# A product-key expert layer mixed with a 2-D Fourier filter: the index of a maximum for two slots at once, three more groups summed on TensorE, fewer loads, a planner with measured figures

## Chip, cores, metric

One core of one Trainium2 chip runs the whole kernel. The metric is device microseconds (us) of one execution. The kernel before takes 991.58 us, the median of 3 runs (990.01 to 991.66).

## The reference, cut to what matters

```python
def _A_ref(x, w_r, w_i):                      # x: 1 x 2048 x 576
    X = rfft2(x) * (w_r + 1j * w_i)
    return irfft2(X)

def _B_ref(x, w_q, k1, k2, u, v):             # 32 heads, 64 x 64 experts
    q = einsum("nd,dhc->nhc", x, w_q)
    s1 = einsum("nhd,ed->nhe", q[..., :128], k1)
    s2 = einsum("nhd,ed->nhe", q[..., 128:], k2)
    e = argmax(s1) * 64 + argmax(s2)          # one expert for each token and head
    act = gelu(einsum("nd,nhd->nh", x, u[e]))
    return einsum("nh,nhd->nd", act, v[e])    # softmax over one candidate is 1

g = sigmoid((x * gate_w).sum(-1))
return g * _A_ref(x, ...) + (1 - g) * _B_ref(x, ...)
```

Inputs and output are float32. Which of the 4096 rows of u and v a token needs is known only after its scores: 2048 tokens x 32 heads x 4608 bytes (a row of u beside a row of v) = 302 MB are gathered.

## The kernel before, in words

The tokens lie in 16 tiles of 128, the heads in 8 chunks of 4. Tiles 0 to 9 (`E_T`) are called early here, tiles 10 to 15 late.

**Scores, 64 slots.** A slot is one chunk and two tiles (`scores`, L402). TensorE (PE) multiplies the transposed x by a matrix that holds w_q times the keys (`build_m`, L381; both are split in a high and a low part, so 28 matmuls of 128 x 512 a slot). VectorE (DVE) takes the maximum of each 64 scores (L427). ScalarE (ACT) makes the sign of maximum minus score (L435), which is 0 at the maximum and 1 elsewhere, and adds 0, 1/4, 2/4 or 3/4 by quarter (L446). DVE then finds the place of the 0: minimum of the two halves (L448, 128 x 512 bf16), of the two quarters (L448, 128 x 256), plus a ramp (L449), minimum over the 16 places left (L451), and the two indices together (L454); ACT writes the row number into `ei` (L455). Each slot does these steps by itself.

**Groups.** A group is one tile and one chunk: 4 gathers (`group`, L480; L487, issued by GpSimd, POOL) fetch 128 rows of 4608 bytes each into a ring of `NG` = 12 buffers, and later also a ring of `NG2` = 1. DVE makes four dot products with x (L496), ACT the gelu (L500), DVE the weights a (L501). The sum over the v rows is done by DVE (L512, L514), or, where `is_d` says so, by PE: ACT writes a diagonal matrix for each weight (L524), PE multiplies it by the v rows (8 matmuls of 128 x 288 a group, two records each in the profile), and DVE or ACT takes the sum out of PSUM (L540, L538). On PE are tiles 1, 4, 8 for chunks 0 to 6, and tiles 10, 12, 14 for all chunks. The 80 early groups run beside the scores, the 48 late ones beside the Fourier part.

**Fourier part.** It starts when the memory of the scores is free (`switch`, L621): 16 folds (L645: symmetric and antisymmetric halves of each row on DVE, then PE), 9 units over frequencies (`unit`, L784: f2 and f4 on PE, the multiplication by w on DVE, L709 to L712, f6 on PE, back into the table `bt` on DVE, L775 to L782), then 16 inversions (`invert`, L808: 6 matmuls of width 289 with `fi`, a copy on ACT, 4 with `krb`), scaled by the gate on ACT (L830, L831) and mixed with the expert sum on DVE (L835).

**Who sets the order.** All instructions are jobs of a planner (`Plan`, L105). Each job has an engine, a guessed duration and a due time; the planner simulates the engines, takes the earliest due job that is ready and has its buffers, and the result is the fixed order of every engine's instructions. On the chip every engine runs its list strictly in order. The due times hang on `TPS` (us for a slot), `LE` (how many slots a group lies behind the scores), `TGS` (pace of late groups) and `FPACE` (pace of the Fourier part). A group may only be placed behind the slot that makes its indices (L601).

Of the kernel before, what the change touches and what calls it, by code (L numbers as in the profile page):

```python
# [32 lines left out]
def _tables():  # L33
# [19 lines left out]
    fwd = np.stack([  # L53
        rows(np.cos, np.arange(0, 128)), rows(np.cos, np.arange(128, 256)), ct,
        -rows(np.sin, np.arange(0, 128)), -rows(np.sin, np.arange(128, 256)), -st,
    ])
    ck = np.full(DF, 2.0)
    ck[0] = ck[-1] = 1.0
    ck /= S * D

    def irows(fn, ks):
        return fn(2 * np.pi * np.outer(ks, k) / D) * ck[ks][:, None]

    ct = z.copy()
    ct[:33] = irows(np.cos, np.arange(256, 289))
    st = z.copy()
    st[64:96] = irows(np.sin, np.arange(256, 288))
    inv = np.stack([
        irows(np.cos, np.arange(0, 128)), irows(np.cos, np.arange(128, 256)), ct,
        irows(np.sin, np.arange(0, 128)), irows(np.sin, np.arange(128, 256)), st,  # L70
# [173 lines left out]
def pe(n):  # L244
    return max(0.25, n * 0.0018)
# [7 lines left out]
def tile_kernel(ctx, tc, xn, xT, wqT, kT, wri, uv, gw, t_kr, t_fi, t_f4, t_f6, t_io, out):  # L253
# [30 lines left out]
    for tag, n in (("cand", 3), ("z", 8), ("b", 8), ("a", 8), ("im", 2), ("fe", 2), ("dg", 4)):  # L284
        ring(tag, "sm", n)
# [3 lines left out]
    for tag, n in (("mh", MB), ("ml", MB), ("mx", 2), ("sg", 2), ("kT", 1), ("ramp", 1)):  # L289
        ring(tag, "sp", n)  # L290
# [65 lines left out]
    def load_x(b, i, at, at2):  # L356
        st = buf("uv", ROW, view=lambda x: x[:, 0, :512])
        ld(load(P * 2048, 2048), at, lambda: nc.sync.dma_start(st.ap, xT[:, i, b * 512 : b * 512 + 512]), [st])
        hi = xts[i if i < 4 else 8][b]
        lo, r = (xts[4 + i][b], 0) if i < 4 else (hi, 64)  # L360
        ac(act(512), at2, lambda: actv(hi.ap, st.ap, AF.Copy), [hi], [st])
        dv(dve(512), at2, lambda: vt(lo.ap[r:], st.ap[r:], hi.ap[r:].bitcast(F32), ALU.subtract), [lo], [st, hi])
# [37 lines left out]
    score_jobs = {}  # L400

    def scores(c, tp, at):  # L402
# [44 lines left out]
        for wd in (E // 2, E // 4):  # L447
            dv(0.07 + wd * 16 / 1920, at, lambda wd=wd: vt(s2()[:, :, :wd], s2()[:, :, :wd], s2()[:, :, wd : 2 * wd], ALU.min), [sg], [])  # L448
        dv(0.2, at, lambda: vt(s2()[:, :, :Q], s2()[:, :, :Q], ramp.ap[:, :Q].unsqueeze(1).to_broadcast([P, 4 * HPC, Q]), ALU.add), [sg], [ramp])  # L449
        im = buf("im", [P, 2, HPC, 2])  # L450
        dv(0.34, at, lambda: nc.vector.tensor_reduce(  # L451
            im.ap.rearrange("p a h b -> p (a h b)"), s2()[:, :, : E // 4], AX.X, ALU.min), [im], [sg])
        fe = buf("fe", [P, 2, HPC])
        dv(0.08, at, lambda: stt(fe.ap, im.ap[:, :, :, 0], float(E), im.ap[:, :, :, 1], op0=ALU.mult, op1=ALU.add), [fe], [im])  # L454
        ac(0.18, at, lambda: actv(ei[tp][:, :, 4 * c : 4 * c + 4], fe.ap, AF.Copy, scale=float(E)), [("ei", tp, c)], [fe])  # L455
# [24 lines left out]
    def group(t, c, at, ahead, gate_by=()):  # L480
        rows = []
        for k in range(HPC):
            g = buf(("uv", "uv2"), ROW)
            h = c * HPC + k

            def go(g=g, h=h):
                on("POOL", nc.gpsimd.indirect_dma_start(  # L487
                    out=g.ap.rearrange("p a d -> p (a d)"), out_offset=None, in_=uv,
                    in_offset=bass.IndirectOffsetOnAxis(ap=ei[t // 2][:, t % 2, h : h + 1], axis=0)))
# [89 lines left out]
    for s in range(NCH * 8):  # L579
# [65 lines left out]
    def fold(t, at):  # L645
        x = xs[t]
        f = buf("f5", [P, ND * P])
        ac(0.17, at, lambda: actv(f.ap[:, 0:385:384], x.ap[:, 0:1].to_broadcast([P, 2]), AF.Copy), [(f, 0)], [x])  # L648
# [15 lines left out]
    def f2(q, at):  # L664
        p = psum()

        def go():
            for r in range(2):
                for n, i in enumerate(((0, 1, 2), (3, 4, 2))[r]):
                    mm(p.ap[:, r, :DF], BT.ap[:, i, :, q], fi[0].ap[:, 3 * r + n, :], start=n == 0, stop=n == 2)  # L670

        plan("PE", 6 * pe(DF), at, go, [p], [fi[0], (BT, "q", q)] + [(BT, "in", t, i) for t in range(NT) for i in range(2)])
# [4 lines left out]
    def turns(k, at):  # L677
        t4 = buf("t4", [P, 3, P])
        t6 = buf("t6", [P, 5, P])
        ld(load(P * 1024, 1024), at - 8, lambda: nc.sync.dma_start(t4.ap[:, 0:2, :], t_f4[k]), [(t4, 0)])  # L680
# [249 lines left out]
```

## Time and profile before

| | |
|---|---|
| median of 3 runs | 991.58 us |
| the profiled execution's own time | 1001.24 us |
| its span, first to last instruction | 999.5 us |
| busy: PE, DVE, ACT, POOL | 90%, 92%, 51%, 57% of the span |
| mean granted clock of PE | 0.965 |
| moved by DMA | 348.39 MB, of it 302.02 MB gathers |
| first gather issued, last gather issued | 36.67 us, 979.74 us |
| scores end on PE, first fold on PE | 601.8 us, 628.6 us |
| first inversion on PE | 862.7 us |

The profiled execution took 1.0% longer than the median. Where a row of the profile says "x16 | 13.5, 751 | 1.6", the group has 16 instructions, was busy for 13.5 us, one of them took 751 ns, and its engine was idle for 1.6 us just before them. In a timeline a row gives the start, the length, the engine, the line, and in brackets how long the engine had been idle and what ended that. DVE overlaps the end of one instruction with the start of the next, so what one costs in a full queue is read from start to start and not from its length.

### The profile page before, as it was taken

How to read it: one execution, taken by the hardware profiler on the slowest of the kernel's cores; microseconds unless marked ns; L12 is line 12 of the kernel's file. 1: busy time of each engine (PE TensorE's matmuls, PEld its weight loads, DVE VectorE, ACT ScalarE, POOL GpSimd, SP SyncE). 2: the span in 40 equal slices, each digit the busy share in tenths (PEclk: the TensorE clock that was granted, in tenths of full speed). 3: DMA queues.
4: the chain of work that ended last, by engine and by line, in shares of the span. 5: the costliest groups of instructions: out<-in, count | busy, mean ns of one | idle time of the engine just before them, and what ended most of it. 6: DMA issues, size and time to landing. Idle time of an engine off the chain costs nothing. (4 is left out here: it accounts for less than half of the span.)

```text
span 999.5 us, 14406 instructions
## 1 busy us (share of the span) xinstructions
PE 904.4 (90%) x4208; PEld 735.8 (74%) x4208; DVE 916.7 (92%) x2255; ACT 514.6 (51%) x1877; POOL 574.4 (57%) x516
## 2 busy tenths in 40 slices
PE   8997999999999999999998990777999998899993
PEld 7885888878877888887877880665777776677762
DVE  3996999999999999999999999999999999977776
ACT  3874676676666576676666664522212222233331
POOL 0354656565656565755657566476655565676662
PEclk9997999999999999999999996889999999899998
DMA  9987999998989999998999799889999999999994
GB/s 336 336 286 301 349 361 367 358 352 305 392 309 361 371 344 332 395 345 328 386 360 330 291 394 378 340 312 389 394 357 351 357 353 321 349 390 414 398 359 192
DMA packets 93246, 348.39 MB, mean 349 GB/s; under 512 B 10480, under 2 KB 13296, under 8 KB 93168
## 3 DMA queue, kind: packets, MB, share of 16 engines
q0 software_dynamic: 73728, 302.02, 80.9%
q1 hardware_dynamic: 19440, 45.45, 12.3%
q8 instruction: 34, 0.56, 0.2%
q14 instruction: 44, 0.36, 0.1%
HBM read 342.71 MB, written 4.72 MB: 348 GB/s over the span
## 5 line engine op out<-in xcount | busy, mean ns | idle before, releaser
L487 POOL DMA_INDIRECT uv<-uv,ei x512 | 574.2, 1121 | 406.2 <-PE p L313 133.3
L313 PE MATMUL p<-mh,xt 128*128 128x512 f32 x1152 | 383.3, 402 | 9.1 <-ACT sg L435 7.3
L435 ACT ACTIVATE sg<-p,mx 128x64 bf16<-128x64 f32 x1024 | 225.8, 352 | 78.1 <-DVE mx L427 55.7
L514 DVE SCALAR_TENSOR_TENSOR xn<-uv,a,xn 128x576 f32<-128x576 f32 x322 | 262.0, 814 | 1.5
L313 PEld LDWEIGHTS p<-mh,xt 128*128 128x128 f32 x1152 | 218.4, 190 | 59.5 <-ACT sg L435 7.7
L313 PE MATMUL p<-ml,xt 128*128 128x512 f32 x640 | 253.2, 396 | 0.0
L496 DVE SCALAR_TENSOR_TENSOR uv<-uv,xn 128x576 f32<-128x576 f32 x320 | 236.3, 749 | 8.7 <-DMA uv<-uv,ei 6.8
L313 PE MATMUL p<-uv,dg 128*128 128x288 f32 x720 | 194.0, 425 | 29.3 <-ACT dg L524 22.5
L313 PEld LDWEIGHTS p<-uv,dg 128*128 128x128 f32 x720 | 140.8, 199 | 77.9 <-ACT dg L524 29.3
L496 DVE SCALAR_TENSOR_TENSOR uv<-uv,xl 128x576 f32<-128x576 f32 x192 | 141.5, 751 | 0.2
L313 PEld LDWEIGHTS p<-ml,xt 128*128 128x128 f32 x640 | 121.6, 190 | 26.6
L500 ACT ACTIVATE b<-z 128x4 f32<-128x4 f32 x128 | 26.4, 206 | 204.9 <-DVE uv L496 171.4
L313 PE MATMUL p<-fi,bt 128*128 128x289 f32 x384 | 97.7, 408 | 4.4 <-DVE t L710 3.0
L313 PEld LDWEIGHTS p<-fi,bt 128*128 128x128 f32 x384 | 83.5, 242 | 16.5 <-issue 3.7
L313 PEld LDWEIGHTS p<-kT,uv 128*128 128x128 f32 x640 | 77.8, 195 | 7.9 <-issue 4.8
L313 PE MATMUL p<-kT,uv 128*128 128x128 f32 x640 | 78.5, 279 | 5.0 <-DMA uv<-wqT 5.0
L427 DVE TENSOR_REDUCE mx<-p 128x16 f32<-128x1024 f32 x64 | 77.5, 1211 | 3.2 <-PE p L313 3.0
L313 PE MATMUL p<-t,t 128*128 128x289 f32 (+2 forms) x384 | 73.8, 362 | 5.9 <-issue 3.4
L446 ACT ACTIVATE sg<-sg 128x256 bf16<-128x256 bf16 x192 | 72.3, 427 | 1.2
L313 PEld LDWEIGHTS p<-t,t 128*128 128x128 f32 (+1 forms) x384 | 54.1, 165 | 23.9 <-issue 10.7
L524 ACT ACTIVATE dg<-ident,a 128x128 f32<-128x128 f32 x180 | 57.6, 393 | 17.7 <-DVE a L501 14.8
L313 PE MATMUL p<-kr,f 128*128 128x128 f32 x160 | 23.0, 301 | 31.5 <-ACT f L648 26.8
(86 smaller groups left out, 612.1 us busy)
## 6 DMA issues: line engine op xcount, KB each, us to landing
uv<-wqT SPq DMA_DIRECT2D x40, 512.0 KB
uv<-uv,ei POOLq DMA_INDIRECT x512
uv<-xT SPq DMA_DIRECT2D x20, 256.0 KB
w<-wri SPq DMA_DIRECT2D x16, 289.0 KB
out<-xn SPq DMA_DIRECT2D x16, 288.0 KB
xn<-xn SPq DMA_DIRECT2D x10, 288.0 KB
t<-t_f SPq DMA_DIRECT2D x18, 128.0 KB
fi<-t_fi SPq DMA_DIRECT2D x2, 867.0 KB
```

The lines of the kernel that those rows point to most:

```text
L313: after("PE", nc.tensor.matmul(*args, **kw))
L427: dv(dve(1024, True), at, lambda: nc.vector.tensor_reduce(mv.ap[:, 2 * tp : 2 * tp + 2, :], ps.ap.rearrange("p a (g e) -> p a g e", e=E), ...
L435: on("ACT", actv(sg.ap[:, j, g, :], ps.ap[:, j, g * E : g * E + E], AF.Sign, bias=mv.ap[:, 2 * tp + j, g : g + 1], scale=-1.0))
L446: ac(act(256), at, lambda b=b: actv(s2()[:, :, b * Q : b * Q + Q], s2()[:, :, b * Q : b * Q + Q], AF.Copy, bias=b / 4), [sg], [])
L487: on("POOL", nc.gpsimd.indirect_dma_start(out=g.ap.rearrange("p a d -> p (a d)"), out_offset=None, in_=uv, in_offset=bass.IndirectOffsetOn ...
L496: dv(0.68, at, lambda k=k, g=rows[k]: stt(g.ap[:, 0, :], g.ap[:, 0, :], 1.0, x.ap, op0=ALU.mult, op1=ALU.mult, accum_out=z.ap[:, k : k + 1 ...
L500: ac(0.18, at - 9, lambda: actv(b.ap, z.ap, AF.Gelu_apprx_tanh), [b], zk, table="gelu")
L514: dv(0.73, at, lambda v=v, s=s: stt(y.ap, v(), s(), y.ap, op0=ALU.mult, op1=ALU.add), [y], [(rows[k], 1), a])
L524: ac(0.3, at - 9, lambda k=k, dg=dg: actv(dg.ap, ident, AF.Copy, scale=a.ap[:, k : k + 1]), [dg], [a, "ident"])
```

## The change

- **Index.** The minimum of the halves of a slot goes to a new tile `sq` that holds two slots; the other four steps (minimum of quarters, ramp, minimum over 16 places, putting together) are done once for two slots, at twice the size, and one `ei` tile covers 4 tiles. A group now waits for the second slot of its pair.
- **PE sums.** `is_d` drops its condition on the chunk: the last groups of tiles 1, 4 and 8 are summed on PE too.
- **Loads.** One Fourier table `fi` in place of a forward and an inverse one (867 KB less); signs and scales move to instructions that were there, and one small scaling of the gate is new. The last rows of x transposed are loaded once and not twice (16 x 256 KB and 4 x 128 KB in place of 20 x 256 KB, estimated from the shapes), and the second half of x comes in loads of double width. The turning factors f4 and f6 of a frequency are one load of 256 KB in place of two of 128 KB.
- **Buffers and planner.** `NG2` is 2, `LE` 4.8 (was 2.8), `FPACE` 1.4 (was 1.7), and PE's guessed cost of a matmul is 0.01 + 0.00168 n us.

```diff
 def pe(n):
-    return max(0.25, n * 0.0018)
+    return 0.01 + n * 0.00168
...
+    def load_x(b, i, at, at2, n=1):
+        st = buf("uv", ROW, view=lambda x: x.rearrange("p a d -> p (a d)")[:, : n * 512])
+        h = P if i < 4 else E
+        src = lambda: xT[:, i, b * 512 : (b + n) * 512] if i < 4 else x5[:, b * 512 : (b + n) * 512]
...
-        for wd in (E // 2, E // 4):
-            dv(0.07 + wd * 16 / 1920, at, lambda wd=wd: vt(s2()[:, :, :wd], s2()[:, :, :wd], s2()[:, :, wd : 2 * wd], ALU.min), [sg], [])
-        dv(0.2, at, lambda: vt(s2()[:, :, :Q], s2()[:, :, :Q], ramp.ap[:, :Q].unsqueeze(1).to_broadcast([P, 4 * HPC, Q]), ALU.add), [sg], [ramp])
-        im = buf("im", [P, 2, HPC, 2])
-        dv(0.34, at, lambda: nc.vector.tensor_reduce(
-            im.ap.rearrange("p a h b -> p (a h b)"), s2()[:, :, : E // 4], AX.X, ALU.min), [im], [sg])
...
+        if tp % 2 == 0:
+            halves[:] = [buf("sq", [P, 2, 4 * HPC, E // 2], BF16)]
+        sq = halves[0]
+        k = tp % 2
+        dv(0.07 + 512 / 1920, at, lambda: vt(sq.ap[:, k], s2()[:, :, : E // 2], s2()[:, :, E // 2 :], ALU.min), [(sq, k)], [sg])
+        if k == 0:
+            return
+        q2 = lambda: sq.ap.rearrange("p s g e -> p (s g) e")
+        dv(0.07 + 512 / 1920, at, lambda: vt(q2()[:, :, :Q], q2()[:, :, :Q], q2()[:, :, Q:], ALU.min), [sq], [(sq, 0), (sq, 1)])
+        dv(0.07 + 512 / 1920, at, lambda: vt(q2()[:, :, :Q], q2()[:, :, :Q], ramp.ap[:, :Q].unsqueeze(1).to_broadcast([P, 8 * HPC, Q]), ALU.add), [sq], [ramp])
+        im = buf("im", [P, 4, HPC, 2])
+        dv(0.06 + 512 / 960, at, lambda: nc.vector.tensor_reduce(
+            im.ap.rearrange("p a h b -> p (a h b)"), q2()[:, :, :Q], AX.X, ALU.min), [im], [sq])
...
-            if cc * 8 + t // 2 > s or (t >= 8 and cc * 8 + 7 > s):
+            if cc * 8 + t // 4 * 2 + 1 > s or (t >= 8 and cc * 8 + 7 > s):
...
-NG2 = 1
-LE = 2.8
+NG2 = 2
+LE = 4.8
...
-FPACE = 1.7
+FPACE = 1.4
...
-    return t % 2 == 0 if t >= NE else t in (1, 4, 8) and c < NCH - 1
+    return t % 2 == 0 if t >= NE else t in (1, 4, 8)
```

The change moves instructions in the planned order. Line numbers of the changed kernel differ by a few (L427 is now L419, L496 is L495, L313 is L299).

On DVE, amid the scores, the index steps of one slot before (`sg`, `im` and `fe` are its tiles; `uv` with `z` is a dot product):

```order
L448 TENSOR_TENSOR sg_888<-sg_888 128x16x32
L496 SCALAR_TENSOR_TENSOR uv_882,z_962<-uv_882,xn_125 128x576
L448 TENSOR_TENSOR sg_888<-sg_888 128x16x16
L427 TENSOR_REDUCE mx_282<-p_192_873 128x16
L449 TENSOR_TENSOR sg_888<-sg_888,ramp_228 128x16x16
L467 TENSOR_TENSOR lc<-mx_282 128x6x4
L451 TENSOR_REDUCE im_1015<-sg_888 128x16
L496 SCALAR_TENSOR_TENSOR uv_902,z_962<-uv_902,xn_125 128x576
L454 SCALAR_TENSOR_TENSOR fe_1025<-im_1015 128x8
```

And now, from the second slot of a pair on:

```order
L443 TENSOR_TENSOR sq_701<-sg_721 128x512
L500 SCALAR_TENSOR_TENSOR a_806<-b_790,sw 128x4
L495 SCALAR_TENSOR_TENSOR uv_678,z_808<-uv_678,xn_116 128x576
L447 TENSOR_TENSOR sq_701<-sq_701 128x32x16
L495 SCALAR_TENSOR_TENSOR uv_689,z_808<-uv_689,xn_116 128x576
L448 TENSOR_TENSOR sq_701<-sq_701,ramp_225 128x32x16
L450 TENSOR_REDUCE im_834<-sq_701 128x32
L495 SCALAR_TENSOR_TENSOR uv_734,z_808<-uv_734,xn_116 128x576
L453 SCALAR_TENSOR_TENSOR fe_849<-im_834 128x16
```

Ten instructions for two slots (five each) have become six: one minimum of the halves for each slot, and one each of the other four, which stand behind the second slot.

On DVE near the start, what stands before the first dot product (`p` is PSUM: `p_105` holds the scores of the third slot; `gz` is a gate sum):

```order
L427 TENSOR_REDUCE mx_282<-p_105_336 128x16
L373 SCALAR_TENSOR_TENSOR uv_192,gz<-xn_125,uv_192 128x576
L362 TENSOR_TENSOR xt_3_22_491<-uv_253,xt_3_6_472 128x512
L373 SCALAR_TENSOR_TENSOR uv_192,gz<-xn_127,uv_192 128x576
L496 SCALAR_TENSOR_TENSOR uv_442,z_509<-uv_442,xn_115 128x576
L373 SCALAR_TENSOR_TENSOR uv_192,gz<-xn_129,uv_192 128x576
```

And now (`p_106` is the fourth slot, `p_110` the fifth, `fe` the first index of all):

```order
L450 TENSOR_REDUCE im_543<-sq_385 128x32
L419 TENSOR_REDUCE mx_277<-p_106_420 128x16
L453 SCALAR_TENSOR_TENSOR fe_554<-im_543 128x16
L443 TENSOR_TENSOR sq_561<-sg_502 128x512
L419 TENSOR_REDUCE mx_277<-p_110_507 128x16
L466 TENSOR_TENSOR cand_594<-mx_277 128x24
L470 TENSOR_TENSOR cand_594<-cand_594 128x24
L495 SCALAR_TENSOR_TENSOR uv_568,z_622<-uv_568,xn_112 128x576
```

The first dot product stood behind the maximum of the third slot; it now stands behind that of the fifth, and the first index behind that of the fourth.

On PE, the end of the list before (`fi` and `krb` are matmuls of an inversion, `dg` those of a group's sum):

```order
L313 MATMUL p_1428_9061<-fi_1189_6645,bt_6676 128x289 x6
L313 MATMUL p_1430_9082<-t_1429_9076,krb_6647 128x289 x4
L313 MATMUL p_1733_8570<-uv_8979,dg_9106 128x288 x2
L313 MATMUL p_1733_8570<-uv_8988,dg_9108 128x288 x2
L313 MATMUL p_1733_8570<-uv_9001,dg_9114 128x288 x2
L313 MATMUL p_1733_8570<-uv_9004,dg_9116 128x288 x2
L313 MATMUL p_1733_8570<-uv_9068,dg_9150 128x288 x2
L313 MATMUL p_1733_8570<-uv_9080,dg_9152 128x288 x2
L313 MATMUL p_1733_8570<-uv_9089,dg_9158 128x288 x2
L313 MATMUL p_1733_8570<-uv_9092,dg_9160 128x288 x2
```

And now:

```order
L299 MATMUL p_1394_8928<-t_1393_8904,krb_6396 128x289 x4
L299 MATMUL p_1396_8939<-fi_6381,bt_6430 128x289 x6
L299 MATMUL p_1398_8955<-t_1397_8953,krb_6396 128x289 x4
L299 MATMUL p_1701_8345<-uv_8823,dg_8965 128x288 x2
L299 MATMUL p_1701_8345<-uv_8830,dg_8967 128x288 x2
L299 MATMUL p_1701_8345<-uv_8847,dg_8971 128x288 x2
L299 MATMUL p_1701_8345<-uv_8864,dg_8973 128x288 x2
```

Two groups stood behind the last inversion, now one does. Behind the last matmul of f6 there were 10 groups on PE in all, now 9. On DVE, 430 of the 512 dot products stood before the last multiplication by w, now 439; before the first fold 308 stood, now 296.

More of the change, by code (lines that the diff above doesn't have):

```diff
@@ L47, in _tables @@
     z = np.zeros((P, DF))
+    c0 = rows(np.cos, np.arange(0, 128))
+    c0[0] *= 0.5
     ct = z.copy()
@@ L52, in _tables @@
     st[64:96] = rows(np.sin, np.arange(256, 288))
[L53 to L70, printed above, removed]
+    fi = np.stack([
+        c0, rows(np.cos, np.arange(128, 256)), ct,
+        rows(np.sin, np.arange(0, 128)), rows(np.sin, np.arange(128, 256)), st,
     ])
@@ L282, in ring @@
         sizes[tag] = n
-    for tag, n in (("cand", 3), ("z", 8), ("b", 8), ("a", 8), ("im", 2), ("fe", 2), ("dg", 4)):
+    for tag, n in (("cand", 3), ("z", 8), ("b", 8), ("a", 8), ("im", 1), ("fe", 2), ("dg", 4)):
         ring(tag, "sm", n)
@@ L288, in tile_kernel @@
     ring("p2", "ps", 4)
-    for tag, n in (("mh", MB), ("ml", MB), ("mx", 2), ("sg", 2), ("kT", 1), ("ramp", 1)):
+    for tag, n in (("mh", MB), ("ml", MB), ("mx", 2), ("sg", 2), ("sq", 1), ("kT", 1), ("ramp", 1)):
         ring(tag, "sp", n)
@@ L334, in tile_kernel @@
     ident = pp.tile([P, P], F32, tag="ident", name="ident")
-    ei = [pp.tile([P, 2, H], U32, tag=f"ei{i}", name=f"ei{i}") for i in range(NT // 2)]
+    ei = [pp.tile([P, 4, H], U32, tag=f"ei{i}", name=f"ei{i}") for i in range(NT // 4)]
     gz = pp.tile([P, NT], F32, tag="gz", name="gz")
@@ L400, in tile_kernel @@
     score_jobs = {}
+    halves = []
     def scores(c, tp, at):
@@ L488, in go @@
                     out=g.ap.rearrange("p a d -> p (a d)"), out_offset=None, in_=uv,
-                    in_offset=bass.IndirectOffsetOnAxis(ap=ei[t // 2][:, t % 2, h : h + 1], axis=0)))
-            plan("POOL", 1.13, at - ahead, go, [(g, 0), (g, 1)], [("ei", t // 2, c)], move=1.65, after=gate_by)
+                    in_offset=bass.IndirectOffsetOnAxis(ap=ei[t // 4][:, t % 4, h : h + 1], axis=0)))
+            plan("POOL", 1.13, at - ahead, go, [(g, 0), (g, 1)], [("ei", t // 4, c)], move=1.55, after=gate_by)
             rows.append(g)
@@ L566, in tile_kernel @@
     for i in range(ND):
-        load_x(2, i, 15, 24)
+        load_x(2, i, 15, 24, 2)
     for t in E_T[4:]:
         load_xn(t, "xn", 16 + t)
-    for i in range(ND):
-        load_x(3, i, 34, when(3))
     for t in E_T:
@@ L669, in go @@
                 for n, i in enumerate(((0, 1, 2), (3, 4, 2))[r]):
[L670 to L672 removed]
+                    mm(p.ap[:, r, :DF], BT.ap[:, i, :, q], fi.ap[:, 3 * r + n, :], start=n == 0, stop=n == 2)
+        plan("PE", 6 * pe(DF), at, go, [p], [fi, (BT, "q", q)] + [(BT, "in", t, i) for t in range(NT) for i in range(2)])
         return p
```

115 lines of the change are left out of this document (56 added, 59 removed).

## Prediction

> **What bounds the kernel now.** I read the page, the stretches of 50 us, the waits, the timelines of DVE and PE and the groups by line, in this order.
>
> ```profile
> span 999.5 us, 14406 instructions
> DMA packets 93246, 348.39 MB, mean 349 GB/s; under 512 B 10480, under 2 KB 13296, under 8 KB 93168
> ```
>
> ```profile
> core 0: us, PE busy (x) PEld busy (x) DVE busy (x) ACT busy (x) POOL busy (x), PEclk, DMA share, GB/s
> 0.00:50.00 50.00, 45.03 (x245) 39.10 (x246) 31.73 (x71) 30.31 (x89) 8.67 (x12) 1.00 0.94 336
> 350.00:400.00 50.00, 49.89 (x241) 40.86 (x240) 49.93 (x123) 35.01 (x142) 30.47 (x27) 1.00 0.94 338
> 600.00:650.00 50.00, 19.73 (x128) 17.41 (x127) 49.73 (x127) 26.81 (x102) 28.16 (x24) 0.73 0.94 360
> 850.00:900.00 50.00, 46.54 (x184) 35.34 (x185) 40.72 (x100) 15.85 (x44) 34.37 (x33) 0.93 0.98 370
> 900.00:950.00 50.00, 50.00 (x207) 38.87 (x206) 36.09 (x84) 17.46 (x47) 30.45 (x28) 1.00 1.02 405
> ```
>
> Columns are busy time and count of each engine, then PE's granted clock, the share of the DMA engines and their rate. From 100 to 850 us DVE is busy for 94% or more of each stretch (49.93 of 50 us in one of these). DMA stands at 0.9 to 1.0 nearly everywhere. PE seems as full, but its matmuls overlap, so I look at who waits:
>
> ```profile
> POOL uv L487 <- PE p L313: 133.3, 55, 9.5
> PE p L313 <- ACT f L648: 26.8, 1, 26.8
> DVE uv L496 <- DMA uv<-uv,ei: 6.8, 10, 1.2
> ```
>
> DVE waited for gathers for 6.8 us in the whole run; the gathers themselves wait for free buffers. PE has one large hole, 26.8 us, at the passage to the Fourier part:
>
> ```profile
> 601.44 0.40 PE L313 MATMUL p<-ml,xt 128*128 128x512 f32 x1
> 628.63 9.41 PE L313 MATMUL p<-kr,f 128*128 128x128 f32 x60 [26.79 <-ACT f L648]
> ```
>
> ```profile
> 618.24 1.22 DVE L427 TENSOR_REDUCE mx<-p 128x16 f32<-128x1024 f32 x1
> 627.62 0.48 DVE L649 TENSOR_TENSOR f<-xn 128x319 f32<-128x319 f32 x1
> ```
>
> PE hands over its last scores at 601.8, DVE reads them at 618.2 and starts the folds at 627.6. So DVE bounds the kernel up to the Fourier part and, by the stretches, to about 850. Behind that PE is full (50.00 of 50 us) until 973:
>
> ```profile
> 862.68 6.21 PE L313 MATMUL p<-fi,bt 128*128 128x289 f32 x24 [0.73 <-ACT bt L761]
> 953.66 6.02 PE L313 MATMUL p<-fi,bt 128*128 128x289 f32 x24
> 963.42 4.04 PE L313 MATMUL p<-uv,dg 128*128 128x288 f32 x16
> 971.13 2.22 PE L313 MATMUL p<-t,krb 128*128 128x289 f32 x8 [0.74 <-ACT t L819]
> 975.12 4.15 PE L313 MATMUL p<-uv,dg 128*128 128x288 f32 x16 [1.77 <-ACT dg L524]
> 984.64 5.84 PE L313 MATMUL p<-uv,dg 128*128 128x288 f32 x16 [5.38 <-ACT dg L524]
> ```
>
> There it waits twice (1.77 and 5.38 us) for the weights of the last two groups, and 9.0 us after its last matmul (990.5) the span ends.
>
> **The change, part by part.** *Index.* DVE's price is read from start to start:
>
> ```profile
> 77.27 0.42 DVE L448 TENSOR_TENSOR sg<-sg 128x512 bf16<-128x512 bf16 x1
> 77.60 0.41 DVE L451 TENSOR_REDUCE im<-sg 128x16 f32<-128x256 bf16 x1
> 77.93 0.28 DVE L448 TENSOR_TENSOR sg<-sg 128x256 bf16<-128x256 bf16 x1
> 78.13 0.16 DVE L454 SCALAR_TENSOR_TENSOR fe<-im 128x8 f32<-128x8 f32 x1
> 78.21 0.53 DVE L512 TENSOR_SCALAR xn<-uv,a 128x576 f32<-128x576 f32 x1
> 78.66 0.28 DVE L449 TENSOR_TENSOR sg<-sg,ramp 128x256 bf16<-128x256 bf16 x1
> 78.86 0.81 DVE L514 SCALAR_TENSOR_TENSOR xn<-uv,a,xn 128x576 f32<-128x576 f32 x1
> 79.59 0.41 DVE L451 TENSOR_REDUCE im<-sg 128x16 f32<-128x256 bf16 x1
> ```
>
> The minimum of halves takes 0.33, the reduction 0.33, the minimum of quarters 0.20, the putting together 0.08, the ramp 0.20: 1.14 us a slot. Twice the size makes 0.33 of each 0.20 (the row of 512 says so). For the reduction two lengths are in the trace:
>
> ```profile
> L427 DVE TENSOR_REDUCE mx<-p 128x16 f32<-128x1024 f32 x64 | 77.5, 1211 | 3.2 <-PE p L313 3.0
> L451 DVE TENSOR_REDUCE im<-sg 128x16 f32<-128x256 bf16 x64 | 26.2, 410 | 0.0
> ```
>
> 768 elements more take 801 ns, so 256 more take 0.27, and it becomes 0.60. New is 0.33 + (0.33 + 0.33 + 0.60 + 0.08) / 2 = 1.00 us a slot, 0.14 less, **9 us** over 64 slots. By the lengths (417, 284, 284, 410 and 158 ns by their groups) it would be 0.30 a slot, 19 us; that is the upper bound, and I keep to start to start, since DVE is never idle here. The Trainium skill (VectorE: DVE Perf Modes, section on the TRN2 errata) gives each instruction a measured fixed cost of about 150 cycles at 0.96 GHz, and four instructions less for two slots would then be worth about 20 us, an estimate. The rows agree with it as a length (512 and 256 elements differ by 133 ns, which leaves 151 ns at zero) but not as a price in a full queue, where 0.07 us is left.
>
> *Three groups to PE.* Twelve sums of 0.73 us (78.86 to 79.59) leave DVE, 8.8 us; three additions from PSUM come:
>
> ```profile
> L540 DVE TENSOR_TENSOR xn<-p,xn 128x576 f32<-128x576 f32 x18 | 13.5, 751 | 1.6 <-PE p L313 1.5
> L496 DVE SCALAR_TENSOR_TENSOR uv<-uv,xn 128x576 f32<-128x576 f32 x320 | 236.3, 749 | 8.7 <-DMA uv<-uv,ei 6.8 <-issue 1.3
> L373 DVE SCALAR_TENSOR_TENSOR uv<-xn,uv 128x576 f32<-128x576 f32 x10 | 7.5, 752 | 0.1
> L362 DVE TENSOR_TENSOR xt<-uv,xt 128x512 fp32r<-128x512 f32 x16 | 10.8, 687 | 12.4 <-ACT xt L361 12.4
> ```
>
> Their lengths less the 0.08 of overlap that the rows above show are 0.67 for such an addition, 0.67 for a dot product and for a gate sum, 0.60 for a correction of x. So DVE has **6.8 us** less in all. PE gets 3 x 4 us (the 16 records at 963.42). By the order two of the three groups lie behind the first fold, in a stage where PE was free for 27 us, which hides them; in the scores one costs PE 4 of the 16 us by which it is ahead there.
>
> *The start.* A group must now wait for two slots.
>
> ```profile
> 36.67 1.07 POOL L487 DMA_INDIRECT uv<-uv,ei  x1 [36.22 <-ACT cand L472]
> ```
>
> ```profile
> 29.61 1.23 DVE L427 TENSOR_REDUCE mx<-p 128x16 f32<-128x1024 f32 x1
> 42.76 0.75 DVE L496 SCALAR_TENSOR_TENSOR uv<-uv,xn 128x576 f32<-128x576 f32 x1
> ```
>
> The first dot product came 6.1 us after the first gather. Between the maximum of the second slot (29.61) and the first index DVE now has 20.9 us of work in the order: 10 gate sums at 0.68, 12 corrections of x at 0.60 (some came later before), 3 maxima at 1.13, 2 corrections of the weights at 0.60, and 2.4 of index and weights. That puts the first gather at about 51.4 and the first dot product at 57.5. Beside it stand some 1.7 us of work, so DVE idles for about 4.5 us; I take **4 us** lost, between 0 (the same work is gone later) and 9 (the next groups come one by one).
>
> *Where it lands.* I add these prices up over the rows of the order. Up to the first fold DVE has 27 us less: 9 of the index, 12 dot products (8.1) and 14 sums (10.2) that now stand later, less 0.7 for an addition. With 4 lost, the first fold moves from 627.6 to about 605. PE's lead of 16 us covers most of that; PE must gain the rest from its waits, which may fail by up to 7 us. From there to the last multiplication by w DVE has 20.4 us more: 21 dot products, 6 sums, 2 additions, 4 weights. The same stage took 227.1 us for 209.8 us of such work:
>
> ```profile
> 854.68 0.76 DVE L709 TENSOR_TENSOR t<-p,w 128x578 f32<-128x578 f32 x1
> ```
>
> At the same ratio 230.2 us take 249, so that row stays at 854, **no gain** there, between -7 (all that DVE saves, with nothing lost; the first rival) and +10 (the rivals with late gathers or longer units).
>
> *The end.* From the first inversion (862.7) to the span's end were 136.8 us: 16 tiles at 5 us (6.0 for the first matmuls of two, 2.1 for the last ones of each), ten groups of 4 us (the order has 10 behind the last f6), 9.0 us of end, and waits of 7 to 8 us. Now there are nine groups, and one of them alone stands behind the last inversion, its dot products ahead of it on DVE. That removes 4 us of PE and most of the 7.2 us of waits: **-10 us**, between -4 and -11. What is late next is the chain behind the last matmul, 9 us as before.
>
> *Loads.* 867 KB and about 512 KB less are 1.4 MB of 348.39, 4 us of DMA at 349 GB/s, and lie beside DVE's work: nothing by themselves, up to 4 us if DMA is the bound. Folding signs into other instructions costs nothing; one scaling of 16 columns costs DVE 0.1 us. The second buffer of the late ring only lets gathers go earlier. Double loads of x take buffers that nothing else wants at 25 to 35 us.
>
> Sum: 0 up to 854, -10 behind: span 989.5, or 0.990 of the profiled execution with the 1.7 us that lie around its span (1001.24). The median of the runs lies 1.0% lower than that execution; 0.990 x 991.58 = **982 us**.
>
> **The rivals.**
>
> *Every DVE saving counts* (20%). No loss at the start and none in the Fourier part: 9 + 6.8 less 9.2 us of group work that moves from the end to the front is -6.6 at the last multiplication, and -10 behind: -16.6, so 975. For it: DVE idles nowhere from 100 to 850. Against it: at 0.95 or more DMA has little left to give earlier gathers.
>
> *The pace of the gathers decides, and the late start is passed on: slower* (14%). 512 gathers went from 36.67 to here:
>
> ```profile
> 979.74 1.10 POOL L487 DMA_INDIRECT uv<-uv,ei  x1 [0.30 <-issue]
> ```
>
> one each 1.845 us. If that pace holds, a start 14.7 us later ends 14.7 us later; 4 us of loads come off: +10.7, so about 1001. For it: DMA's share, 0.91 to 1.02. Against it: 33 gathers went in the 50 us from 850, one each 1.52, and DVE waited for gathers for 6.8 us in all. It decides from where DVE asks for more than that: my first stage needs 308 gathers (296 and a ring of 12) in 553 us, one each 1.80, my second 143 in 249, one each 1.74, both faster than now, the second with the factors and w beside it. If DVE's row of dot products shows tens of us of waits for gathers, this is it.
>
> *The bytes decide* (13%). The mean rate of 349 GB/s is what the transfers can do, and what is loaded less is the whole gain: 4 us, 987.6. The stretch at 405 GB/s from 900 on speaks against it. The Trainium skill (DMA: Bandwidth & Descriptors, section Bandwidth) says that for transfers between HBM and SBUF the HBM side binds at about 358 GB/s for a core; by that rule the whole 347 MB take no less than 969 us, an estimate, and little but the bytes would count. The windows of 370 and 405 GB/s do not agree with it.
>
> *The Fourier part gets longer* (13%). It holds 21 more dot products and runs its units in a new order, paced by 1.4; if each of its nine units takes 1 us more than the ratio says, the 10 us of the end are gone: 991, no change. For it: buffers of the units stay four. Against it: DVE had work of groups to fill waits with, and has more now.
>
> **How the numbers follow.** My forecast, 982, has 40%. The range must leave out no more than 2 in 10: it goes from 970 (the first rival, with half of the 10 us by which the index could be worth more) to 997 (half of the slower one). A measurement of this kernel tells a change from none at about 0.2%, 2 us. Faster by more than that: 0.39 of my case, the first rival's 0.20 and 0.11 of the third, 0.70 in all. Within it: 0.10 of the fourth, 0.02 of the third and 0.01 of the second, 0.13. Slower: 0.13 of the second, 0.03 of the fourth and 0.01 of mine, 0.17.
>
> **What would show it.** Right: the steps of the index at 0.33, 0.33, 0.60 and 0.08 from start to start, once for two slots; first gather near 51; first fold near 605, the hole of PE before it near 13 us; the last multiplication by w near 854; from the first inversion to the end 127 us, without the waits of 1.77 and 5.38. Wrong: DVE's waits for gathers above 20 us in all; a first fold behind 615; a wait of PE at the end for weights as before; units that follow each other slower than 24 us.

## The result, and the profile after

The changed kernel takes 976.69 us (median of 4 runs, 975.66 to 977.22), the kernel before 991.62 us (4 runs): the ratio is 0.9855, 95% interval 0.9839 to 0.9872, 14.9 us less. The forecast was 982, 9.6 less.

The profiled execution of before that the prediction worked with lies 9.6 us above the median of the runs. A second one (run b_same below) lies at 992.55 us, so it is the better partner for comparing places, and I use it from here on. First the span and the DMA totals of after, from its page:

```profile
span 973.9 us, 14306 instructions
DMA packets 90893, 346.97 MB, mean 356 GB/s; under 512 B 10240, under 2 KB 10752, under 8 KB 90816
```

Then the stretches from the start to DVE's first fold, from there to shortly behind the start of the last multiplication by w (the second stretch of before likewise), and from the first inversion to the end; columns as in the prediction. After:

```profile
0.00:595.61 595.61, 575.07 (x2784) 476.67 (x2784) 561.50 (x1300) 401.06 (x1522) 345.10 (x309) 0.99 0.94 350
595.61:842.80 247.19, 217.12 (x992) 175.55 (x992) 239.49 (x594) 68.75 (x224) 156.98 (x144) 0.95 0.99 381
848.78:973.90 125.12, 113.86 (x464) 87.66 (x464) 91.20 (x214) 40.89 (x107) 69.27 (x62) 0.98 0.87 334
```

Before (run b_same):

```profile
0.00:618.73 618.73, 575.15 (x2768) 473.54 (x2768) 587.69 (x1468) 408.97 (x1552) 360.96 (x320) 0.98 0.94 353
618.73:846.90 228.17, 201.79 (x934) 165.51 (x935) 220.53 (x539) 65.39 (x211) 132.48 (x122) 0.94 0.95 348
853.04:990.80 137.76, 120.88 (x480) 92.39 (x480) 101.78 (x237) 42.13 (x113) 78.13 (x71) 0.95 0.90 349
```

The third number after the length is DVE's busy time, and the length less that is DVE's idle time. In the first stretch DVE works 26.2 us less (587.69 to 561.50) and idles 3.1 more (31.0 to 34.1): the first fold comes 23.1 us earlier. In the second it works 19.0 us more and idles as before (7.6 and 7.7), so 4.1 of the 23.1 are left at the last multiplication by w (842.17 and 846.24). Behind the first inversion the end is 12.6 us shorter.

### The profile page after: what moved, and what is told of

The parts are those of the page before. It is cut to its first block, busy times and chain, and to the rows that moved or that the text cites. A ratio compares the mean times of both kernels' runs of the same rounds, so it can differ in the third digit from the quotient of the medians.

```text
span 973.9 us, 14306 instructions
## 1 busy us (share of the span) xinstructions
PE 909.2 (93%) x4256; PEld 741.6 (76%) x4256; DVE 898.1 (92%) x2119; ACT 511.6 (53%) x1855; POOL 574.7 (59%) x516
## 3 DMA queue, kind: packets, MB, share of 16 engines
q1 hardware_dynamic: 17088, 44.03, 12.6%
## 5 line engine op out<-in xcount | busy, mean ns | idle before, releaser
L299 PE MATMUL p<-mh,xt 128*128 128x512 f32 x1152 | 379.0, 399 | 0.0
L427 ACT ACTIVATE sg<-p,mx 128x64 bf16<-128x64 f32 x1024 | 226.8, 349 | 105.1 <-DVE mx L419 103.1
L299 PEld LDWEIGHTS p<-mh,xt 128*128 128x128 f32 x1152 | 216.9, 188 | 48.7
L299 PE MATMUL p<-ml,xt 128*128 128x512 f32 x640 | 251.8, 393 | 0.0
L513 DVE SCALAR_TENSOR_TENSOR xn<-uv,a,xn 128x576 f32<-128x576 f32 x310 | 250.9, 810 | 1.0
L495 DVE SCALAR_TENSOR_TENSOR uv<-uv,xn 128x576 f32<-128x576 f32 x320 | 235.7, 748 | 11.3 <-DMA uv<-uv,ei 11.2
L299 PE MATMUL p<-uv,dg 128*128 128x288 f32 x768 | 200.6, 416 | 20.3 <-ACT dg L523 15.9
L299 PEld LDWEIGHTS p<-uv,dg 128*128 128x128 f32 x768 | 146.5, 194 | 66.4 <-ACT dg L523 21.0
L299 PEld LDWEIGHTS p<-ml,xt 128*128 128x128 f32 x640 | 120.7, 189 | 26.8
L495 DVE SCALAR_TENSOR_TENSOR uv<-uv,xl 128x576 f32<-128x576 f32 x192 | 140.8, 749 | 0.3 <-DMA uv<-uv,ei 0.2
L299 PE MATMUL p<-fi,bt 128*128 128x289 f32 x384 | 101.1, 416 | 9.5 <-DVE t L704 4.4
L299 PEld LDWEIGHTS p<-fi,bt 128*128 128x128 f32 x384 | 84.1, 243 | 24.2 <-issue 8.2
L299 PEld LDWEIGHTS p<-kT,uv 128*128 128x128 f32 x640 | 77.8, 195 | 8.4 <-issue 4.7
L299 PE MATMUL p<-kT,uv 128*128 128x128 f32 x640 | 78.6, 279 | 5.3 <-DMA uv<-wqT 5.2
L419 DVE TENSOR_REDUCE mx<-p 128x16 f32<-128x1024 f32 x64 | 77.7, 1214 | 5.6 <-PE p L299 5.6
L438 ACT ACTIVATE sg<-sg 128x256 bf16<-128x256 bf16 x192 | 74.4, 429 | 1.1
L523 ACT ACTIVATE dg<-ident,a 128x128 f32<-128x128 f32 x192 | 61.4, 393 | 15.2 <-DVE a L500 15.0
L299 PE MATMUL p<-tw,t 128*128 128x256 f32 (+1 forms) x256 | 40.3, 332 | 4.5 <-DVE t L705 2.2
L299 PEld LDWEIGHTS p<-tw,t 128*128 128x128 f32 (+1 forms) x256 | 29.6, 150 | 15.7 <-issue 7.9
L299 PE MATMUL p<-kr,f 128*128 128x128 f32 x160 | 24.3, 316 | 14.4 <-DVE f L646 12.9
```

What stands on the lines that cost most here:

```text
L299: after("PE", nc.tensor.matmul(*args, **kw))
L419: dv(dve(1024, True), at, lambda: nc.vector.tensor_reduce(mv.ap[:, 2 * tp : 2 * tp + 2, :], ps.ap.rearrange("p a (g e) -> p a g e", e=E), ...
L427: on("ACT", actv(sg.ap[:, j, g, :], ps.ap[:, j, g * E : g * E + E], AF.Sign, bias=mv.ap[:, 2 * tp + j, g : g + 1], scale=-1.0))
L438: ac(act(256), at, lambda b=b: actv(s2()[:, :, b * Q : b * Q + Q], s2()[:, :, b * Q : b * Q + Q], AF.Copy, bias=b / 4), [sg], [])
L495: dv(0.68, at, lambda k=k, g=rows[k]: stt(g.ap[:, 0, :], g.ap[:, 0, :], 1.0, x.ap, op0=ALU.mult, op1=ALU.mult, accum_out=z.ap[:, k : k + 1 ...
L513: dv(0.73, at, lambda v=v, s=s: stt(y.ap, v(), s(), y.ap, op0=ALU.mult, op1=ALU.add), [y], [(rows[k], 1), a])
```

## The experiments

Each run's ratio is to the runs of before on the same chip. Three groups of four ran, each on a chip of its own; before took 990.36 us in the first (b_same to b_plan), 1006.94 in the second (a_le to a_bytes) and 991.93 in the third (after_again to a_tB).

### b_same: before once more

No edit.

> The kernel before, unchanged, for a second profiled execution. The first one took 1001.24 us where the runs have a median of 991.6, and DVE stood idle in it for 4.77 and 3.18 us at 84 and 95 us. If those two idle times belong to that execution alone, this one shows a time near 991, no such idle times and a first fold near 619.5 us. If they belong to the kernel, they are here again, the first fold is at 627, and the difference from the median lies somewhere else.

992.55 us. DVE's last maximum and first fold:

```profile
609.35 1.22 DVE L427 TENSOR_REDUCE mx<-p 128x16 f32<-128x1024 f32 x1
618.73 0.48 DVE L649 TENSOR_TENSOR f<-xn 128x319 f32<-128x319 f32 x1
```

The first fold is 8.9 us earlier than in the execution of the prediction, and the idle times of 4.77 and 3.18 us are not there. They belonged to that one execution.

### b_index, a_le, b_index_le: the new index and the planner's 4.8

b_index is before with the new index only (the diff's lines on sq, ei, im, fe and the condition in the planner's loop). The other two turn one number, and b_index_le also takes a line on the ring of t2 from after:

```
a_le:        -LE = 4.8   +LE = 2.8     (on after)
b_index_le:  -LE = 2.8   +LE = 4.8     (on b_index)
             -return buf(("t2", "xn"), list(shape))
             +return buf(("t2", "xn") if shape[1] == D else "t2", list(shape))
```

> Before, with the index for two slots at once and nothing else. By the rows of its order at their start-to-start prices DVE has 6.7 us less up to the first fold, 10.8 less from there to the last multiplication by w, and 8.5 more behind it (8.9 less in all). Theory that DVE's work sets the time up to the last multiplication by w and PE with the groups left sets the rest: 4 us lost at the start, so about 13 earlier at the last multiplication by w, 5 to 9 later behind it: 983 to 988 us. Every DVE saving counts: 983. Gathers' pace or bytes decide: no gain, 991 (bytes) to 1000 (pace, since the first gather is some 10 to 15 us later).

> After, with 2.8 slots for 4.8 between a group's index and its turn, as before the change. Theory that the planner's turn must leave room for the second slot of a pair: groups come to their turn about a slot before their indices and rows are there, DVE idles in the scores as in the run of before with the new index alone (there 47 us more than before): 1010 to 1025 us, and DVE's waits for gathers, weights and PE rise by 30 us or more. Theory that only DVE's work counts: its rows are the same in sum (14 us more up to the first fold, 14 less behind it): 977 to 980.

> Before, with the new index and 4.8 slots for 2.8 (and the second of two rings that a tile may take left out, which no tile took). Theory that the turn was too early for pairs: the 47 us of the run without the 4.8 go. DVE's rows are 23 us less up to the first fold, 6 more up to the last multiplication by w, 8.5 more behind it, 4 are lost at the start: 983 to 988 us. Theory that the pairing itself stalls DVE (both slots' index at once, one buffer of halves): 1020 or more still.

b_index: 1037.78 us, ratio 1.049 (1.0463 to 1.0517), slower by 47 us where 983 to 988 was expected; my theory as I had put it missed by far. a_le: ratio 1.0418 (1.0376 to 1.0461). b_index_le: 0.9952 (0.992 to 0.9985), which is 986.9 on the scale of 991.6 and inside 983 to 988 (the interval, 983.7 to 990.1, is wider).

Up to the last multiplication by w DVE idles 86.0 us in b_index and 38.7 in b_same, 47 more; its work there is 11.4 us less, and the end is 8.5 us longer, with eleven groups left to PE in place of ten. DVE's largest waits in b_index, by what it waited for (us in total, times, longest; the first two are 10.2 and 18.2 us in b_same):

```profile
DVE uv L504 <- DMA uv<-uv,ei: 37.5, 39, 3.1
DVE a L509 <- ACT b L508: 23.3, 31, 2.8
DVE xn L548 <- PE p L313: 12.8, 9, 2.9
```

And why the gathers were late, in POOL's queue of the same run:

```profile
206.66 1.01 POOL L495 DMA_INDIRECT uv<-uv,ei  x1 [7.62 <-ACT ei L463]
...
289.86 0.94 POOL L495 DMA_INDIRECT uv<-uv,ei  x1 [12.35 <-ACT ei L463]
```

POOL stands still before a gather until ACT has written the index. In a_le such stops of 12 to 13 us come at 209, 292, 374, 459, 540 and 618 us, one in each chunk of eight slots. Summed over the runs, POOL's waits for the index as ACT writes it (us in total, times, longest) are in b_index

```profile
POOL uv L495 <- ACT ei L463: 60.9, 7, 12.3
```

in a_le

```profile
POOL uv L486 <- ACT ei L454: 86.2, 8, 13.4
```

in b_index_le

```profile
POOL uv L495 <- ACT ei L463: 18.5, 5, 6.0
```

and in after

```profile
POOL uv L486 <- ACT ei L454: 8.2, 5, 2.8
```

The planner gives a group its turn LE slots behind its place in the count. With one index for two slots the first slot of a pair gets its index a slot later, and 2.8 is then too early: POOL's queue is in order, so one gather that waits holds up all behind it, and DVE runs dry. This is shown, in both directions: taking the 4.8 from after costs some 6% (1.0418 against the 0.984 to 0.9855 of after, which was measured on other chips), giving it to b_index takes away what b_index lost.

### b_groups and b_plan: the other parts alone

```
b_groups:  -return t % 2 == 0 if t >= NE else t in (1, 4, 8) and c < NCH - 1
           +return t % 2 == 0 if t >= NE else t in (1, 4, 8)
b_plan:    NG2 1 -> 2, LE 2.8 -> 4.8, FPACE 1.7 -> 1.4, move 1.65 -> 1.55,
           pe(n): max(0.25, n * 0.0018) -> 0.01 + n * 0.00168
```

(`move` is the planner's guess for the transfer of a gather; it belongs to the change as well.)

> Before, with the last groups of tiles 1, 4 and 8 summed on PE and nothing else. By the rows of its order DVE has 3.7 us less up to the first fold, 11.5 less up to the last multiplication by w and 8.5 more behind it (6.7 less in all). Theory that DVE sets the time up to there and PE with the groups left the rest: 15 earlier at the last multiplication by w, 8 to 12 later behind it: 984 to 989 us. Every DVE saving counts: 985. Bytes or the gathers' pace decide: 991 to 992, no change.

> Before, with the planner's numbers alone changed (late ring 2, 4.8 for 2.8, units paced by 1.4 for 1.7, the measured cost of matmuls and 1.55 for 1.65 per gather). DVE's rows are the same in sum: 16.4 us less up to the first fold, 25.5 more up to the last multiplication by w, 9.2 less behind it. Theory that DVE's work sets the time up to the last multiplication by w: that row comes 9 to 11 us later, and the end behind it is some 10 us shorter: 990 to 993 us, no change. If the gain of the whole change came from the planner's numbers (work moved out of the end, where PE is full), this run alone shows most of it, 980 or less.

b_groups: 997.95 us, ratio 1.0082 (1.0055 to 1.0108). b_plan: 995.21, ratio 1.0057 (1.0033 to 1.0081). The first was to be 2 to 8 us faster and is 7.6 slower; the second was to be no change, and is 4.8 slower. Their stretches, b_groups:

```profile
618.16:839.70 221.54, 196.47 (x943) 163.17 (x944) 209.13 (x513) 64.40 (x209) 129.47 (x115) 0.96 0.95 349
845.53:992.20 146.67, 125.62 (x496) 95.60 (x496) 111.15 (x259) 43.68 (x119) 87.62 (x79) 0.95 0.92 354
```

b_plan:

```profile
0.00:610.55 610.55, 575.80 (x2768) 476.27 (x2768) 571.23 (x1430) 406.51 (x1552) 345.91 (x308) 0.98 0.93 345
610.55:862.20 251.65, 207.33 (x955) 168.29 (x956) 244.75 (x600) 66.22 (x216) 159.30 (x144) 0.93 0.98 373
868.07:993.50 125.43, 113.84 (x464) 87.58 (x464) 91.23 (x212) 41.00 (x107) 67.92 (x61) 0.97 0.87 336
```

b_plan's end is 125.4 us long, like that of after (125.1), with neither the new index nor the three groups in it. So the whole gain at the end comes from the planner's numbers, which leave nine groups to PE there. It is given back earlier: the groups that leave the end are done ahead of it. b_groups leaves eleven groups at the end (146.7 us). Its profiled execution (993.98 us) is the fastest of its six; 4 us of its loss are not in it and stay unexplained.

### a_dve and a_bytes: more work for DVE, more bytes

```
a_dve:    (scores, even slots from 8 on) the line that writes sq.ap[:, k] twice
a_bytes:  +if s >= 8 and s % 3 == 0:
          +    plan("SP", 0.06, at, ... nc.sync.dma_start(out[d], xs[d].ap) ...)
```

> After, with the minimum of halves done twice in 28 of the 64 slots, which changes no value: 28 x 0.336 = 9.4 us more for DVE in the scores, and nothing else. Theory that DVE's start-to-start work sets the time up to the last multiplication by w: 985 to 987, and the first fold 9 us later. Bytes or the gathers' pace decide: 977.

> After, with 19 more transfers of 288 KB from tiles of x to the output's place during the scores (5.6 MB, overwritten later by the real output). Bytes decide: 5.6 MB at 356 GB/s, 15.7 us, so 992. Theory that DVE sets the time: the transfers take the 2 to 5 per cent that the DMA engines have left there, 977 to 980; if gathers get late by them, DVE's waits for gathers rise above the 11.6 us of after by as much as the time does.

a_dve: ratio 1.0024 (0.9991 to 1.0057), 1008.40 us; a_bytes: 0.9942 (0.9914 to 0.997), 1000.05 us. After itself did not run on this chip. If its ratio there is the 0.984 to 0.9855 of the other chips, 9.4 us of DVE's work cost some 17 us, and 5.6 MB cost 9 to 10. Without that assumption the two runs can be compared with each other: up to the last multiplication by w DVE works 10.8 us more in a_dve (811.5 against 800.7) and idles 2.2 less (58.3 against 60.5), and a_dve takes 8.4 us more; by the bytes it would have been 15.7 the other way. So added work of DVE shows in the time. Both idle 16 to 19 us more than after (41.8); whether the chip or the new order does that, no run separates. a_bytes is a weak test, though: nothing held its transfers back, and all 19 went between 27 and 46 us, where after moved 269 GB/s and a_bytes 363:

```profile
0.00:50.00 50.00, 44.99 (x246) 39.20 (x247) 31.33 (x62) 30.32 (x93) 0.20 (x4) 1.00 1.00 363
```

There they pushed back the loads of the start; whether bytes matter in the scores it cannot say.

### after_again, a_groups_old, a_index_old: one part taken out

```
a_groups_old:  -t in (1, 4, 8)    +t in (1, 4, 8) and c < NCH - 1
a_index_old:   the index of each slot by itself, as in before
```

> The changed kernel itself, for runs on the same chip as the other three of this group (the group before it met a chip on which the kernel before took 1007 us). Its ratio to before is 0.9855 on record; near that if the chip scales both kernels alike. If the changed kernel depends more on what is slow there, nearer to 1.

> After, with the last groups of tiles 1, 4 and 8 summed on DVE again. By its order DVE has 3.5 us more up to the first fold and 3.3 more up to the last multiplication by w; nine groups are left to PE behind the first inversion, as in after. Theory that DVE's work sets the time: 6.7 to 7.5 us more than after on the same chip. Alone on top of before these groups made the kernel 7.6 us slower; if that is their own cost, this run is as fast as after or some us faster.

> After, with the index of each slot by itself, and all else as in after (4.8 slots too). By its order DVE has 7.5 us more up to the first fold and 1.4 more up to the last multiplication by w. Theory of the prediction: 9 us more of DVE's work less 4 won back at the start, so 5 us more than after on the same chip. Every DVE saving counts: 9 more. The late first gather costs more than the index saves: the same or faster than after.

after_again: 976.82 us, ratio 0.984 (0.9814 to 0.9866). a_groups_old: 991.47, ratio 0.9992 (0.9973 to 1.0011). a_index_old: 992.49, ratio 0.9992 (0.9972 to 1.0013). Each part taken out costs 15 to 16 us, not 7 and 5: all that the change had brought. Both runs still have the new loads, which were never run alone; so the loads do not bring the gain by themselves. Stretches of a_groups_old:

```profile
0.00:604.89 604.89, 573.92 (x2768) 475.33 (x2768) 565.78 (x1305) 397.45 (x1516) 350.25 (x310) 0.99 0.94 348
604.89:860.00 255.11, 214.33 (x960) 173.40 (x960) 243.16 (x600) 67.46 (x218) 156.67 (x143) 0.91 0.96 364
```

and of a_index_old:

```profile
0.00:611.52 611.52, 582.84 (x2784) 481.01 (x2784) 567.66 (x1427) 405.13 (x1553) 345.69 (x308) 0.99 0.93 342
611.52:861.50 249.98, 217.65 (x991) 176.20 (x992) 241.18 (x596) 69.65 (x228) 155.29 (x144) 0.95 0.97 373
```

DVE's busy time up to the last multiplication by w is 801.0 us in after (561.50 + 239.49), 808.9 in a_groups_old and 808.8 in a_index_old: 7.9 and 7.8 more, close to the 6.8 and 8.9 of the orders. Its idle time is 41.8, 51.1 and 52.7. The rest, 9 to 11 us, is idle time. In a_index_old it is the wait for gathers:

```profile
DVE uv L488 <- DMA uv<-uv,ei: 20.5, 27, 2.4
```

against 11.4 in after; in a_groups_old it is spread over gathers (16.2) and the weights from ACT:

```profile
DVE a L500 <- ACT b L499: 17.5, 19, 3.1
```

against 10.7. Both profiled executions lie 2 to 3 us above the median of their runs, which does not account for it. What makes the idle time grow is not settled: each edit makes the planner write a new order, and no run holds the order still while the work changes. Each of these idle times is also from one execution; two executions of before, with one order, had 46.2 and 38.7 us, and two of after 41.8 and 41.9.

### a_tB: another choice of tiles

```
-t % 2 == 0 if t >= NE      +t in (10, 11, 12) if t >= NE
```

> After, with tile 11 summed on PE in place of tile 14: eight groups' sums go from DVE to PE in the Fourier part (DVE 11.8 us less before the last multiplication by w), and eight from PE to DVE at the end, where PE then has no group left behind the first inversion (36 us of PE less) and DVE 11.7 us more. Theory that DVE sets the time up to the last multiplication by w and PE behind it: 12 us earlier there, and the end, bound by DVE then (105 us of work and waits of 10 to 15), 5 to 10 us shorter: 13 to 22 us less than after on the same chip. Rival: two tiles' sums hold two of the four PSUM buffers through the Fourier part and its units wait: no gain or slower.

977.31 us, ratio 0.9842 (0.9814 to 0.987): no gain over after. The end became shorter, as expected, and the Fourier part longer:

```profile
598.25:864.00 265.75, 245.37 (x1136) 200.07 (x1136) 229.81 (x593) 83.52 (x265) 166.24 (x153) 0.97 0.99 376
872.16:978.30 106.14, 80.30 (x320) 61.74 (x320) 99.36 (x210) 28.37 (x66) 58.85 (x50) 0.87 0.85 332
```

DVE has 9.7 us less to do there than in after but idles 35.9 us where it idled 7.7. PE is the one that is full now:

```profile
700.00:750.00 50.00, 49.56 (x221) 39.99 (x221) 34.62 (x94) 16.45 (x53) 32.18 (x29) 1.00 0.99 378
```

where after has

```profile
700.00:750.00 50.00, 46.30 (x207) 37.21 (x207) 48.84 (x118) 10.70 (x36) 32.00 (x30) 0.99 1.00 385
```

PE is busy for 49.56 of 50 us (46.30 in after), DVE for 34.62 (48.84). The rival had the outcome, but the trace speaks for the matmuls of the eight groups (32 us at 4 each) and not for the PSUM buffers: PE idles only 20.4 us of this stretch (30.1 in after), and beside the wait for the first folds and 11.6 us for the weights, its waits sum to 5.1 us (14.0 and 14.3 in after). A wait for a buffer would be among these 5.1. That the buffers shaped the planned order is not excluded. No version here beats after.

## Why the prediction was right, point by point

The result lies in the range of 970 to 997, and nearer to the first rival's 975 than to the forecast's 982. The forecast missed some 4 us at the last multiplication by w and some 2 at the end; both are taken up below.

**Index: right, slightly too much.** In DVE's timeline of after, the steps stand between other work:

```profile
385.00 0.41 DVE L447 TENSOR_TENSOR sq<-sq 128x512 bf16<-128x512 bf16 x1
385.34 0.81 DVE L513 SCALAR_TENSOR_TENSOR xn<-uv,a,xn 128x576 f32<-128x576 f32 x1
386.07 0.41 DVE L448 TENSOR_TENSOR sq<-sq,ramp 128x512 bf16<-128x512 bf16 x1
386.40 0.75 DVE L495 SCALAR_TENSOR_TENSOR uv<-uv,xn 128x576 f32<-128x576 f32 x1
387.08 0.67 DVE L450 TENSOR_REDUCE im<-sq 128x32 f32<-128x512 bf16 x1
387.68 0.74 DVE L495 SCALAR_TENSOR_TENSOR uv<-uv,xn 128x576 f32<-128x576 f32 x1
388.35 0.17 DVE L453 SCALAR_TENSOR_TENSOR fe<-im 128x16 f32<-128x16 f32 x1
388.44 0.74 DVE L539 TENSOR_TENSOR xn<-p,xn 128x576 f32<-128x576 f32 x1
```

From start to start 0.34, 0.33, 0.60 and 0.09, as forecast, and 0.33 for the minimum of the halves (L443, 383.94 to 384.27): 1.02 us a slot instead of 1.14, 8 us in all. The estimate from the fixed cost of about 150 cycles in the Trainium skill (VectorE: DVE Perf Modes, section on the TRN2 errata) was 20 us. The page gives that cost for the duration of a single instruction; as a price in a full queue it does not show here.

**Three groups: right.** 21 additions from PSUM at 0.67. In the scores PE took its one group and handed over its last scores at 583.70 (row below), 7.3 us earlier than in b_same:

```profile
591.01 0.40 PE L313 MATMUL p<-ml,xt 128*128 128x512 f32 x1
```

It gained that from its waits, as the prediction needed: up to there it idles 9.0 us, 16.3 in b_same.

**The start: right.** The first gather came at 51.68 (51.4 forecast), the first dot product at 56.44 (57.5):

```profile
51.68 1.08 POOL L486 DMA_INDIRECT uv<-uv,ei  x1 [51.23 <-DVE sq L443]
```

```profile
56.44 0.76 DVE L495 SCALAR_TENSOR_TENSOR uv<-uv,xn 128x576 f32<-128x576 f32 x1 [2.15 <-DMA uv<-uv,ei]
59.13 0.76 DVE L495 SCALAR_TENSOR_TENSOR uv<-uv,xn 128x576 f32<-128x576 f32 x1 [1.93 <-DMA uv<-uv,ei]
60.96 0.76 DVE L495 SCALAR_TENSOR_TENSOR uv<-uv,xn 128x576 f32<-128x576 f32 x1 [1.06 <-DMA uv<-uv,ei]
```

These three waits are 5.1 us. In the first 100 us DVE idles 27.5 us, and 20.7 in b_same: the start lost 6.8 us where 4 were taken, inside the stated 0 to 9. Later in the scores 3.7 of them come back, so that over the whole first stretch DVE idles 3.1 us more.

**The first fold: right in the difference.** Forecast 605, measured 595.61; but 8.9 us of that is the odd execution that I started from. Against b_same it is -23.1, forecast -22.6. PE's hole before it, forecast at 13 us:

```profile
583.70 0.40 PE L299 MATMUL p<-ml,xt 128*128 128x512 f32 x1
...
596.34 3.97 PE L299 MATMUL p<-kr,f 128*128 128x128 f32 x17 [12.25 <-DVE f L646]
```

**The last multiplication by w: mis-sized by 3.5 us.** I let the Fourier part grow in proportion, 20.4 us of work making 22, so that nothing would be left there. It made 19.0 (19.0 busy, idle unchanged), since the work itself was 1.4 less than the 20.4 of the sum and what is not work in this stage did not grow with it:

```profile
842.17 0.75 DVE L703 TENSOR_TENSOR t<-p,w 128x578 f32<-128x578 f32 x1
```

It stood at 846.24 in b_same: 4.1 us gained where the forecast had none and the first rival, that every saving counts, 6.6. The sign that I named, units slower than 24 us apart, was badly chosen: from the first to the last of these rows (643.0 to 842.2, eight units on) they are 24.9 us apart, and 22.1 in b_same (669.5 to 846.2). The part is longer by its added work, not by waits.

**The end: right, 2 us too small.** From the first inversion to the end 125.1 us, forecast 127, 137.8 in b_same. Behind the last inversion only one group is left, and no wait for its weights:

```profile
954.03 3.09 PE L299 MATMUL p<-fi,bt 128*128 128x289 f32 x12
957.86 2.22 PE L299 MATMUL p<-t,krb 128*128 128x289 f32 x8 [0.74 <-ACT t L814]
959.91 4.04 PE L299 MATMUL p<-uv,dg 128*128 128x288 f32 x16
```

One group less is 4.0 us, and PE's idle time between the first inversion and its last matmul falls from 7.9 us in b_same to 1.3, 6.6 less. The forecast took every group at 4 us; in b_same the last one, behind its wait, took

```profile
974.78 7.03 PE L313 MATMUL p<-uv,dg 128*128 128x288 f32 x16 [5.38 <-ACT dg L524]
```

7.03 us at a mean granted clock of 0.58, where the last one of after, without a wait, takes 4.04 at 1.00. (In the execution of the prediction it took 5.84, at 0.71.) So with the wait another 3.0 us went that the sum does not have. The chain behind the last matmul became 1.0 us longer (9.95 in place of 8.99).

**The rivals.** The gathers' pace: the start was 15 us later and the end was not, for the 512 gathers went one each 1.76 us (51.68 to 951.25) and not one each 1.845; DVE's waits for gathers stayed at 11.4 us:

```profile
DVE uv L495 <- DMA uv<-uv,ei: 11.4, 15, 2.2
```

It does not bind in after, but it may be near: in a_groups_old and a_index_old these waits were 16.2 and 20.5 us. (The prediction's sum for this rival, 10.7 us on top of 991.6, is 1002 and not 1001; nothing hangs on it.) The bytes: 1.4 MB less are 4 us by the mean rate, and 14.9 were gained; from 650 to 700 us DMA moved

```profile
650.00:700.00 50.00, 40.08 (x160) 30.48 (x160) 48.17 (x118) 13.35 (x38) 36.33 (x33) 0.91 1.03 411
```

411 GB/s, above the 358 at which by the Trainium skill (DMA: Bandwidth & Descriptors, section Bandwidth) the HBM side binds for a core. The same section has 425 GB/s measured for one core with the pair's other core idle; so 358 is no bound here. Whether bytes bind a little below the 976 us of after is not tested: its DMA share was 0.94 and 0.99 in the first two stretches.

**What the prediction did not see.** It treated each part as a price that adds up, with DVE's idle time left as it was. For the whole change that held within 3.1 us (38.7 us of idle up to the last multiplication by w in b_same, 41.8 in after; 46.2 in the execution that it started from). For the parts it did not: in b_plan, a_groups_old and a_index_old the idle time is 46.2, 51.1 and 52.7, and the last multiplication by w, at 842 in after, stands near 860 in all three. And the 4.8, which the prediction only carried along in the order, is what lets the new index be worth anything. As far as the runs tell, being right on the total rests on the planner having found an order with few stalls for just this set of numbers. The forecast had no row to tell that from an order with 10 us more: this part was luck.

## What to carry to other kernels

Price an instruction of a full queue from start to start, and sum it over the order: in after, b_groups, b_plan, a_groups_old and a_index_old the change of DVE's busy time came out within 2 us of it for each stage up to the last multiplication by w. The idle time between is not part of that sum. Where a planner writes the order anew it moved by 3 to 11 us in these five runs, as much as the edits themselves were worth, and in before by 7.5 between two executions of one order; a term for it belongs in the range. Look also at what follows a wait: behind 5.38 us of idle PE a group took 7.03 us here and not 4.04. When a step makes its result available later, look for the number that says when it is needed: in an in-order queue one early turn per chunk cost 47 us.

## What the runs showed that I had not expected

The parts of the change do not add: alone on before they gave +47, +7.6 and +4.8 us, together -14.9, and either of two taken out gives all of it back. The loads, the fourth part, had no run of their own. One kernel ran 1.6% longer on one chip than on two others (1006.94 against 990.36 and 991.93), with 28, 12 and 23 runs. The changed kernel repeats within 1.6 us over nine runs on two occasions (975.66 to 977.27), before within 9.6 over 23 runs.
